# Fourth attention block: eight buffers for transposed P, and products by v ordered in front of MLP products

## The chip, the cores and the metric

The kernel runs on one core of one Trainium2 chip. The metric is the device time of the core in microseconds (us). TensorE does the matrix products, VectorE and ScalarE the elementwise work, GpSimd a few small operations and accumulating stores, and SyncE issues most of the loads and all the DMA transposes. Each engine works through its own queue in the order in which the program was scheduled.

## The reference

Inputs are q, k, v of shape (4, 8, 576, 64) and forget gates f of shape (4, 8, 576). Three layers follow each other:

```python
# 1: causal attention with a decay bias, per batch and head
scores = q @ k.T / 8 + (cum[:, None] - cum[None, :])      # cum = cumsum(log f)
attn = exp(masked scores - row max);  attn /= sum(attn) + 1e-9
x = concat_heads(attn @ v)                                 # (4, 576, 512)
# 2: MLP on the layer norm, with a residual
x = x + max(norm(x) * g @ w1, 0) @ w2                      # 512 -> 2048 -> 512
# 3: gated unit with mixing over positions
u, v = split(max(x @ w_in, 0));  out = (u * (w_spatial @ norm(v) + b)) @ w_out
```

## The kernel before

The 2304 tokens (4 batches of 576) are cut into nine blocks of 256 token columns. Blocks 1 and 2 hold the first 128 positions of two batches each, blocks 3 and 4 positions 128 to 255 of two batches each, blocks 5 to 8 the rest of one batch each, and the ninth column block gathers what is left over. For each block the attention runs, then its normalization, then the MLP. The MLP runs in eight groups of blocks: group 0 for block 1, group 1 for block 2, and so on. Each group has 16 steps, one for each tile of 128 hidden units: the first-layer product of step j into a bank `ph` (L864), a ReLU into `hh` (ScalarE, L875) and the low half `hl` (VectorE, L879), and then the second-layer product of the hidden tile two steps back into `acc` (function `second`, L849). From group 1 on, each product is taken as three fp16 products of high and low halves: 12 matmuls a step in each layer. There are two `ph` banks and three `hh`/`hl` buffers.

The attention of blocks 3 and 4 is `attention1`. Its unit is a head pair and a batch: eight units a block. A unit loads q/k, decay rows and v (L523 to L525), computes scores (L532), a row minimum with the mask (VectorE, L537), the exponential (ScalarE, L539), the reciprocal (L541), normalized P as high and low fp16 halves (L544 and L546), transposes P by one DMA on SyncE's queue (L547, the transposes kept in order among themselves), takes the product by v, 12 matmuls (L555), and writes the result into `xT` (ScalarE, L556). Buffers of each kind come from a dictionary: `BUFS1` for block 3, `BUFS1B` for block 4 (`self.deep` is set before block 4).

The order of the work is made in two stages. `run` gives each step of each block's attention and of each MLP group a time on a common axis and emits them in the order of these times; block 4 (the fourth entry of SPAN, 1.04 to 1.36) is emitted beside group 1 (1.0 to 1.5). Then the scheduler of the language takes the instructions with its own estimates of durations: on each engine, the earliest emitted one that it believes ready. That makes the fixed order of each engine's queue. `self.after(later, earlier)` adds an edge that only constrains this order.

Of the kernel before, what the change touches and what calls it, by code (L numbers as in the profile page):

```python
# [27 lines left out]
SC = 2.0 ** 14  # L28
BUFS = dict(vr=1, vp=2, qk=3, x1=3, x2=3, PT=4, sd=3, st=6, P16=5, xt=1)
BUFS0 = dict(vr=1, qk=1, e=4, diag=2, PT=2, st=4)  # L30
BUFS1B = dict(vr=4, vp=4, qk=4, sd=4, P16=4, PT=3, st=8)
BUFS1 = dict(vr=3, vp=3, qk=3, sd=2, P16=2, PT=2, st=6)
DHE = (0, 0, 0)
MB = dict(xT=4, xh=8, hh=3, y=2)
# [5 lines left out]
AHEAD = 2  # L40
# [39 lines left out]
def f32(ap):  # L80
    return ap.bitcast(F32)
# [7 lines left out]
class Kernel:  # L89
# [422 lines left out]
    def attention1(self, b, xT):  # L512
        nc, at, bufs = self.nc, self.at, BUFS1B if self.deep else BUFS1
        mm = nc.tensor.matmul
        for p in range(NP):
            for n in range(2):
                ph = at.tile([P, 2, 2, 2, P], F16, tag="P16", name="P16", bufs=bufs["P16"])
                PT = at.tile([P, 2, 2, 2, P], F16, tag="PT", name="PT", bufs=bufs["PT"])
                vr = at.tile([P, 2, P], F32, tag="vr", name="vr", bufs=bufs["vr"])
                vp = at.tile([P, 2, 2, P], F16, tag="vp", name="vp", bufs=bufs["vp"])  # L520
                qk = at.tile([66, 2, 3 * P], F32, tag="qk", name="qk", bufs=bufs["qk"])
                h = b * H + 4 * p + n
                nc.sync.dma_start(out=qk[:64], in_=self.qk1[b + n, p, :64])  # L523
                nc.sync.dma_start(out=qk[64:], in_=self.decay1_d[h : h + 3 : 2].rearrange("u r s -> r u s"))
                load = nc.sync.dma_start(out=vr, in_=self.v[b + n, : 2 * P, p * P : (p + 1) * P].rearrange("(t p) d -> p t d", p=P))  # L525
                if n:
                    self.marks.setdefault("second", load)
                vsc = self.parts16(vr, vp[:, 0], vp[:, 1], b + n if self.deep else None)
                yield
                ps = self.bank("s").rearrange("p (u k) -> p u k", u=2)  # L530
                for u in range(2):
                    mm(ps[:, u], lhsT=qk[:, u, :P], rhs=qk[:, u, P:], start=True, stop=True, skip_group_check=True)  # L532
                sd = at.tile([P, 2, 2 * P], F32, tag="sd", name="sd", bufs=bufs["sd"])
                st = at.tile([P, 4], F32, tag="st", name="st", bufs=bufs["st"])
                for u in range(2):
                    mn, sm = st[:, u : u + 1], st[:, 2 + u : 3 + u]
                    nc.vector.tensor_tensor_reduce(  # L537
                        out=sd[:, u], in0=ps[:, u], in1=self.mask[:, 3 * P :], scale=-0.125, scalar=3e38, op0=ALU.add, op1=ALU.min, accum_out=mn)
                    nc.scalar.activation(sd[:, u], sd[:, u], AF.Exp, bias=mn, scale=-1.0, accum_out=sm)  # L539
                nc.scalar.activation(st[:, 2:], st[:, 2:], AF.Copy, bias=1e-9 / SC, scale=1.0 / SC)  # L540
                nc.vector.reciprocal(st[:, 2:], st[:, 2:])  # L541
                for u in range(2):
                    rs, src = st[:, 2 + u : 3 + u], sd[:, u].rearrange("p (t w) -> p t w", w=P)
                    dh, dl = ph[:, u, :, 0], ph[:, u, :, 1]  # L544
                    self.copy(0, dh, src, rs)
                    nc.vector.scalar_tensor_tensor(out=dl, in0=src, scalar=rs, in1=dh, op0=ALU.mult, op1=ALU.subtract)  # L546
                tr = nc.sync.dma_start_transpose(out=PT.rearrange("p u t h w -> p (u t h) w"), in_=ph.rearrange("p u t h w -> p (u t h w)"))  # L547
                self.in_order("tr", tr)
                yield
                pav = self.bank("av")[:, :P]  # L550
                terms = [(kt, vi, pi) for kt in range(2) for vi, pi in ((0, 1), (1, 0), (0, 0))]
                for g, (kt, vi, pi) in enumerate(terms):
                    for u in range(2):
                        us = slice(64 * u, 64 * u + 64)
                        mm(pav[us], lhsT=vp[:, vi, kt, us], rhs=PT[:, u, kt, pi], start=g == 0, stop=g == len(terms) - 1, skip_group_check=True)  # L555
                nc.scalar.activation(xT[:, p, n * P : (n + 1) * P], pav, AF.Copy, scale=vsc)  # L556
                if n == 0:
                    yield
            if p == 1:
                xs = self.mo_sum(xT)  # L560
            elif p == 2:
                nc.vector.tensor_tensor(out=xs, in0=xs, in1=xT[:, 2, :], op=ALU.add)
            yield
        return xs
# [249 lines left out]
    def mlp(self, g, states, y):  # L814
# [19 lines left out]
        def weight(j, c0, right):  # L834

            cs = slice(c0, c0 + P)
            if not g:
                return [(self.wt[:, j + 2, cs], right)]
            h, l = self.pair(j)
            rh, rl = right  # L840
            return [(l[:, cs], rh), (h[:, cs], rl), (h[:, cs], rh)]

        def second(j, hidden, last):
            for m in range(NK):

                bank = m if n > 1 else m // 2
                terms = weight(j, DM + m * P, hidden)
                for e, (a, b) in enumerate(terms):
                    ins = nc.tensor.matmul(acc[m], lhsT=a, rhs=b, start=bank not in clear, stop=last and e == len(terms) - 1, skip_group_check=True)  # L849
                    if bank not in clear:  # L850
                        clear[bank] = ins
                    elif m not in seen and not e:
                        self.after(ins, clear[bank])
                    seen.add(m)

        pend = []
        for i in range(n):
            x = split(i)
        for j in range(NF):
            ph = self.bank("ph")[:, :W]  # L860
            for k in range(NK):
                terms = weight(j, k * P, (xn[k][0][:, :W], xn[k][1][:, :W]) if g else x[:, k, :])
                for e, (a, b) in enumerate(terms):
                    ins = nc.tensor.matmul(ph, lhsT=a, rhs=b, start=k == e == 0, stop=k == NK - 1 and e == len(terms) - 1)  # L864
                    if (g, j, k) == (0, SUMS, 0):
                        self.after(ins, self.marks["sums"])
            if g == 0:
                self.marks["hidden"] = ins
                for i in range(SQ[j - 1] if j else 0, SQ[j]) if j < len(SQ) else ():
                    self.squares(i)  # L870
            hh = mo.tile([P, 2 * TOK], F16, tag="hh", name="hh", bufs=MB["hh"])
            hl = mo.tile([P, 2 * TOK], F16, tag="hl", name="hl", bufs=MB["hh"])[:, :W] if g else None
            hh = hh[:, :W] if g else f32(hh)
            with self.tc.high_priority(1):
                relu = nc.scalar.activation(hh, ph, AF.Relu)  # L875
                if g < 2:
                    self.done.append(relu)
                if g:
                    nc.vector.scalar_tensor_tensor(out=hl, in0=ph, scalar=0.0, in1=hh, op0=ALU.max, op1=ALU.subtract)  # L879
            pend.append((j, (hh, hl) if g else hh, j == NF - 1))  # L880
            if j >= AHEAD:
                second(*pend[j - AHEAD])
            yield
        for args in pend[-AHEAD:]:
            second(*args)
# [400 lines left out]

    def run(self):
        self.setup()
        last = len(BLOCKS)
        ps_cm = self.banks("psum")  # L1290
        self.psum = ps_cm.__enter__()
# [170 lines left out]
        g, begun = self.mlp2(0), 0  # L1462
        for b in range(B):
# [12 lines left out]
            g = after  # L1476
# [57 lines left out]
```

## Time and profile before

| what | value |
|---|---|
| median of 3 runs (lowest, highest) | 764.69 us (762.89, 765.9) |
| profiled execution, its span | 763.16 us, 761.2 us |
| TensorE busy | 739.7 us (97%) |
| VectorE, ScalarE, GpSimd busy | 590.9, 528.8, 67.4 us |
| TensorE busy in 150 to 200 us | 49.64 of 50 us |
| TensorE busy in 250 to 300, in 300 to 350 us | 48.28, 46.36 of 50 us |
| DMA share in 150 to 200, in 300 to 350 us | 0.68, 0.96 |

An engine's busy time counts its instructions, not its waits. Matmuls are pipelined, so a row's busy time can reach into the next row's; the distance between two starts tells how long TensorE was taken. In a timeline row the bracket at the end holds the idle time before the row and what ended it. "x12" merges twelve neighbours of one kind.

### The profile page before, as it was taken

The page shows a single profiled execution, that of the slowest core. Times are in us where ns is not written, and L with a number is a line of the kernel's source. Part 1 is how long each engine was busy: PE and PEld are TensorE (multiplying, and loading weights), DVE is VectorE, ACT ScalarE, POOL GpSimd, SP SyncE. Part 2 cuts the span into 40 slices and gives each one's busy share as a digit, 9 for nine tenths or more (in the row PEclk, how much of TensorE's full clock was granted, in tenths as well). Part 3 has the DMA queues.
Part 4 walks back from the last instruction along what each step waited for, and adds up shares of the span by engine and source line. Part 5 has one row for each costly group of instructions (what it writes and reads, how often), then busy time and mean ns, then how long its engine had stood idle before and what let it go on. Part 6 is the DMA issues. An engine that isn't in the chain of part 4 may idle for free.

```text
span 761.2 us, 16265 instructions
## 1 busy us (share of the span) xinstructions
PE 739.7 (97%) x5912; PEld 567.9 (75%) x5912; DVE 590.9 (78%) x1569; ACT 528.8 (69%) x1320; POOL 67.4 (9%) x102
## 2 busy tenths in 40 slices
PE   8899998999999999999999999999999999999998
PEld 6788887888888877877888888644447678768686
DVE  7899799577599989989869845689456796785854
ACT  6898699576588989879857844587346764664633
POOL 6001100013102010110110100200012000000000
PEclk9999999999999999999999999999999999999999
DMA  8978694466589998988965944831025240100101
GB/s 263 295 269 274 206 266 84 89 171 105 176 167 206 198 220 183 195 189 177 201 144 116 148 84 149 213 132 56 1 22 111 70 125 1 44 21 7 57 2 62
DMA packets 164100, 104.68 MB, mean 138 GB/s; under 512 B 106147, under 2 KB 151299, under 8 KB 164021
## 3 DMA queue, kind: packets, MB, share of 16 engines
q1 hardware_dynamic: 153032, 93.06, 50.3%
q0 software_dynamic: 5376, 5.54, 5.2%
q10 hardware_dynamic: 5612, 5.06, 2.2%
q8 instruction: 46, 0.75, 0.4%
q14 instruction: 34, 0.27, 0.1%
HBM read 64.37 MB, written 15.11 MB: 104 GB/s over the span
## 4 chain that ended last, share of the span: by engine, by line
PE 63%; DVE 11%; ACT 10%; DMA 10%; issue 4%; SPq 2%; DVEq 0%; ACTq 0%
PE ph L864 16%; PE acc L849 12%; PE pb L808 8%; PE pb L809 8%; PE pb L810 8%; DMA raw<-in_moe_w_ch_dram 3%; PE s L359 3%; PE s L849 3%; DMA vr<-in_v_dram 2%; PE av L586 2%; ACT wt L744 2%; ACT P L319 2%; DMA x_d<-xT 2%; DVE P L380 1%; DMA qk<-decay 1%
## 5 line engine op out<-in xcount | busy, mean ns | idle before, releaser
L849 PE MATMUL acc<-hh,wt 128*128 128x256 f16 (+2 forms) x960 | 196.8, 295 | 3.2 <-ACT hh L875 3.2
L864 PE MATMUL ph<-xh,wt 128*128 128x256 f16 (+1 forms) x896 | 185.0, 288 | 2.0 <-DVE hl L879 2.0
L864 PEld LDWEIGHTS <-wt 128*128 128x128 f16 x1344 | 126.9, 98 | 47.4 <-issue 10.2
L849 PEld LDWEIGHTS <-wt 128*128 128x128 f16 x1344 | 128.7, 98 | 44.3 <-issue 5.3
L864 PE MATMUL ph<-xl,wt 128*128 128x256 f16 (+1 forms) x448 | 129.0, 288 | 0.0
L849 PE MATMUL acc<-hl,wt 128*128 128x256 f16 (+1 forms) x416 | 115.8, 281 | 1.1 <-DVE hl L879 1.1
L875 ACT ACTIVATE hh<-ph 128x256 f16<-128x256 f32 (+2 forms) x128 | 50.9, 397 | 45.8 <-PE ph L864 45.5
L879 DVE SCALAR_TENSOR_TENSOR hl<-ph,hh 128x256 f16<-128x256 f32 (+1 forms) x112 | 50.5, 453 | 35.9 <-ACT hh L875 35.7
L319 ACT ACTIVATE P<-sd,st 128x512 f16<-128x512 f32 (+2 forms) x128 | 70.6, 585 | 9.8 <-DVE st L370 6.9
L380 DVE SCALAR_TENSOR_TENSOR P<-sd,st,P 128x384 f16<-128x384 f32 (+2 forms) x96 | 59.2, 634 | 10.5 <-ACT P L319 10.3
L367 ACT ACTIVATE sd<-sd,st 128x384 f32<-128x384 f32 (+2 forms) x80 | 54.6, 682 | 14.4 <-DVE st L363 14.2
L359 PE MATMUL s<-x2z 128*128 128x384 f32 (+3 forms) x128 | 47.8, 382 | 1.9 <-DMA x2z<-decay_d 1.7
L363 DVE CUSTOM_DVE_ANT_0 sd<-s,mask 128x384 f32<-128x384 f32 (+2 forms) x80 | 46.0, 579 | 3.7 <-PE s L359 2.7
L900 POOL DMA_DIRECT2D x_d<-t x36 | 31.9, 1024 | 182.7 <-DVE t L896 153.1
L359 PE MATMUL s<-x 128*128 128x384 f32 (+3 forms) x128 | 41.4, 333 | 0.0
L809 PE MATMUL pb<-wsl,vh 128*128 128x288 f16 x128 | 36.6, 286 | 0.0
L808 PE MATMUL pb<-wsh,vl 128*128 128x288 f16 x128 | 36.6, 286 | 0.0
L810 PE MATMUL pb<-wsh,vh 128*128 128x288 f16 x128 | 36.4, 286 | 0.0
L810 PE MATMUL pb<-gh,woh 128*128 128x288 f16 x128 | 35.0, 286 | 0.0
L809 PE MATMUL pb<-gl,woh 128*128 128x288 f16 x128 | 35.0, 286 | 0.0
L808 PE MATMUL pb<-gh,wol 128*128 128x288 f16 x128 | 33.3, 286 | 0.0
L922 ACT ACTIVATE gh<-u 128x288 f16<-128x288 f32 x32 | 14.0, 437 | 26.5 <-DVE u L1261 26.5
(341 smaller groups left out, 1692.5 us busy)
## 6 DMA issues: line engine op xcount, KB each, us to landing
raw<-in_moe_w_ch_dram SPq DMA_DIRECT2D x32, 512.0 KB
qk<-in_qk_dram SPq DMA_DIRECT2D x32, 448.0 KB
vraw<-in_v_dram SPq DMA_DIRECT2D x5, 1024.0 KB
vr<-in_v_dram SPq DMA_DIRECT2D x16, 320.0 KB
x_d<-t POOLq DMA_DIRECT2D x36, 128.0 KB, 4.3
out_dram<-o SPq DMA_DIRECT2D x32, 144.0 KB
raw<-in_moe_w_in_dram SPq DMA_DIRECT2D x8, 512.0 KB
qk<-in_qk_dram SPq DMA_DIRECT2D x16, 192.0 KB
```

Of the source, the lines that this page charges most:

```text
L319: self.nc.scalar.activation(out, in_, AF.Copy, scale=scale)
L359: nc.tensor.matmul(ps[: R * u + R, : c1 - c0], lhsT=x[:, lo - q0 - R * u : hi - q0], rhs=y[:, c0:c1], start=g == 0, stop=g == len(heads[u] ...
L363: nc.vector.tensor_tensor_reduce(out=sd[:M, c0:c1], in0=ps[:M, : c1 - c0], in1=mask, scale=-0.125, scalar=3e38 if n == 0 else st[:M, n - 1 ...
L367: nc.scalar.activation(sd[:M, :N], sd[:M, :N], AF.Exp, bias=st[:M, n : n + 1], scale=-1.0, accum_out=st[:M, 2:3])
L380: low = nc.vector.scalar_tensor_tensor(out=dl, in0=src, scalar=rs, in1=dh, op0=ALU.mult, op1=ALU.subtract)
L808: first = mm(out, lhsT=al, rhs=bh, start=start, stop=False, **kw)
L809: mm(out, lhsT=ah, rhs=bl, start=False, stop=False, **kw)
L810: mm(out, lhsT=ah, rhs=bh, start=False, stop=stop, **kw)
L849: ins = nc.tensor.matmul(acc[m], lhsT=a, rhs=b, start=bank not in clear, stop=last and e == len(terms) - 1, skip_group_check=True)
L864: ins = nc.tensor.matmul(ph, lhsT=a, rhs=b, start=k == e == 0, stop=k == NK - 1 and e == len(terms) - 1)
L875: relu = nc.scalar.activation(hh, ph, AF.Relu)
L879: nc.vector.scalar_tensor_tensor(out=hl, in0=ph, scalar=0.0, in1=hh, op0=ALU.max, op1=ALU.subtract)
```

## The change

The fourth block gets eight buffers of transposed P in place of three. The last matmul of each of its products by v is remembered. At each MLP step the one remembered last is appended to a list of at most ten; in group 1 the first matmul of the second-layer products is placed behind the oldest entry of the list, that is, the product by v that had been emitted nine steps before. The full diff:

```diff
-BUFS1B = dict(vr=4, vp=4, qk=4, sd=4, P16=4, PT=3, st=8)
+BUFS1B = dict(vr=4, vp=4, qk=4, sd=4, P16=4, PT=8, st=8)
...
                     for u in range(2):
                         us = slice(64 * u, 64 * u + 64)
-                        mm(pav[us], lhsT=vp[:, vi, kt, us], rhs=PT[:, u, kt, pi], start=g == 0, stop=g == len(terms) - 1, skip_group_check=True)
+                        ins = mm(pav[us], lhsT=vp[:, vi, kt, us], rhs=PT[:, u, kt, pi], start=g == 0, stop=g == len(terms) - 1, skip_group_check=True)
+                if self.deep:
+                    self.summed1 = ins
...
-        def second(j, hidden, last):
+        def second(j, hidden, last, trail=()):
...
+                    if m == e == 0 and trail and trail[0] is not None:
+                        self.after(ins, trail[0])
...
             if j >= AHEAD:
-                second(*pend[j - AHEAD])
+                self.trail = [*self.trail, self.summed1][-10:]
+                second(*pend[j - AHEAD], self.trail if g == 1 else ())
...
         self.setup()
+        self.summed1, self.trail = None, []
```

## Rows read from the trace of the kernel before

**Rows 1.** Page, busy us, share of the span, instructions of TensorE
```profile
PE 739.7 (97%) x5912; PEld 567.9 (75%) x5912; DVE 590.9 (78%) x1569; ACT 528.8 (69%) x1320; POOL 67.4 (9%) x102
```
**Rows 2.** Busy time by stretch: stretch, length, each engine, granted clock, DMA share, GB/s
```profile
157.28:179.50 22.22, 21.86 (x181) 18.09 (x179) 21.20 (x76) 20.85 (x72) 2.05 (x2) 1.00 0.62 141
200.00:350.00 150.00, 143.93 (x1294) 117.80 (x1292) 135.98 (x371) 131.60 (x341) 15.43 (x24) 1.00 0.92 188
```
**Rows 3.** TensorE timeline, waits of 200 to 350 us: start, busy, instruction, [idle, releaser]
```profile
218.93 0.27 PE L864 MATMUL ph<-xh,wt 128*128 128x256 f16 x1 [0.71 <-DVE hl L879]
...
268.40 0.30 PE L586 MATMUL av<-PT,vp 128*64 128x320 f16 x1 [1.68 <-DMA PT<-P]
...
301.92 0.27 PE L849 MATMUL acc<-hl,wt 128*128 128x256 f16 x1 [1.11 <-DVE hl L879]
...
324.55 0.30 PE L586 MATMUL av<-PT,vp 128*64 128x320 f16 x1 [1.04 <-DMA PT<-P]
...
348.41 0.41 PE L359 MATMUL s<-x2z 128*128 128x384 f32 x1 [1.49 <-DMA x2z<-decay_d]
```
**Rows 4.** TensorE timeline of the fourth block beside group 1
```profile
157.28 0.27 PE L849 MATMUL acc<-hh,wt 128*128 128x256 f16 x1
...
157.61 1.03 PE L532 MATMUL s<-qk 66*128 66x256 f32 x4
...
172.45 0.53 PE L555 MATMUL av<-PT,vp 128*64 128x128 f16 x12
...
173.68 0.27 PE L849 MATMUL acc<-hh,wt 128*128 128x256 f16 x1
...
184.07 0.53 PE L555 MATMUL av<-PT,vp 128*64 128x128 f16 x12
...
196.80 0.53 PE L555 MATMUL av<-PT,vp 128*64 128x128 f16 x12
```
**Rows 5.** VectorE timeline, low half of P of units 1, 4 and 8
```profile
163.37 0.88 DVE L546 SCALAR_TENSOR_TENSOR P<-sd,st,P 128x256 f16<-128x256 f32 x2 [0.24 <-ACT P L319]
...
171.00 0.88 DVE L546 SCALAR_TENSOR_TENSOR P<-sd,st,P 128x256 f16<-128x256 f32 x2
...
181.48 0.87 DVE L546 SCALAR_TENSOR_TENSOR P<-sd,st,P 128x256 f16<-128x256 f32 x2
```
**Rows 6.** SyncE timeline: transposes of the fourth block, first loads of the fifth
```profile
164.28 1.24 SPq L547 DMA_TRANSPOSE PT<-P  x1
...
169.14 19.90 SPq L547 DMA_TRANSPOSE PT<-P  x6
189.14 1.01 SPq L330 DMA_DIRECT2D qk<-in_qk_dram  x2
```
**Rows 7.** SyncE and TensorE timelines, third block: a transpose and its product
```profile
126.52 1.89 SPq L547 DMA_TRANSPOSE PT<-P  x1
...
130.00 0.53 PE L555 MATMUL av<-PT,vp 128*64 128x128 f16 x12 [0.58 <-DMA PT<-P]
```
**Rows 8.** Waits of SyncE's queue, 150 to 260 us: total us, times, longest
```profile
SPq L547 <- PE av L555: 8.6, 4, 3.0
```
**Rows 9.** ScalarE timeline: a ReLU of group 1, first operands of the fifth block
```profile
165.51 0.36 ACT L875 ACTIVATE hh<-ph 128x256 f16<-128x256 f32 x1
...
199.06 0.94 ACT L319 ACTIVATE x<-qk 128x896 fp32r<-128x896 f32 x1
```
**Rows 10.** TensorE and VectorE timelines: third block's last product, a held subtraction
```profile
151.14 0.53 PE L555 MATMUL av<-PT,vp 128*64 128x128 f16 x12
...
156.97 1.41 DVE L782 TENSOR_TENSOR xT<-xT,av 128x256 f32<-128x256 f32 x4 [1.70 <-DMA x_d<-xT]
```
**Rows 11.** Chain that ended last, in order of time: start, us, work
```profile
135.56 0.97 PE s L532 x4
...
179.65 1.31 PE ph L864 x12
180.96 0.46 PE av L555 x12
```

## The prediction

> **What bounds the kernel now.** I read the page's busy times first. TensorE is busy 739.7 of 761.2 us [rows 1], so all its idle time together is 21.5 us, and no reordering can give back more. The profiled execution took 763.16 us, 1.96 us more than its span; the median of the runs shown is 764.69, so the profiled execution lies 1.5 us (0.2%) below it, near the fastest run.
>
> Then I looked for the part of the idle time that lies where the change can reach, in the busy times by stretch. From the point where the fourth block's scores begin to the end of the MLP group that runs beside it, TensorE is busy 21.86 of 22.22 us: 0.36 us idle. VectorE (21.20) and ScalarE (20.85) are almost as full, because there the fourth block's softmax runs at full speed. From 200 to 350 us, where the four wide attention blocks run, TensorE is busy 143.93 of 150 [rows 2]. TensorE's timeline names the five waits that make up nearly all of these 6.07 us: 0.71, 1.68, 1.11, 1.04 and 1.49, together 6.03, of which 4.21 are waits for DMAs (transposed P twice, rows of x2z once) [rows 3]. So the fourth block itself has nothing to give. A gain has to come from the blocks behind it.
>
> Third, the timeline of the fourth block. TensorE's queue holds its score matmuls from 157.61 on, but its eight products by v stand far behind: the first at 172.45, the fourth at 184.07, the eighth at 196.80, one per MLP step at the end [rows 4]. They wait for nothing there. P of the first unit is finished at 163.37 + 0.88 = 164.25, of the fourth at 171.88, of the eighth at 182.35 [rows 5], and SyncE starts the first transpose at 164.28 [rows 6]. How long a transpose takes until its product can run is seen in the third block, where the product did wait: issued at 126.52, product at 130.00, so 3.5 us [rows 7]. The first product could have run at 167.8 and the eighth near 185.9. The order of the queue, not the data, makes them late.
>
> What these late products hold back is SyncE. With three buffers of transposed P, the fourth transpose waits for the first product, and so on: four waits of 8.6 us in all [rows 8]. The last six transposes occupy SyncE's in-order queue from 169.14 to 189.04, and the first load of the fifth block (L330) stands behind them at 189.14 [rows 6]. ScalarE starts on the fifth block's operands at 199.06, just after the last product [rows 9].
>
> **The change part by part.** *Eight buffers.* There are eight units (four head pairs, two batch halves), so no transpose waits for a product any more. SyncE is through when P of the eighth unit is ready and its transpose issued: 182.35 + 1.3 = 183.7 in place of 189.0, so the loads of the fifth block can be issued 5.4 us earlier. One unit of transposed P is 2 KB per partition, so the pool grows by 10 KB, and by the order of allocation the fourth block's q/k tiles come to lie on tiles of the third block's pool. Their first load then waits for the third block's last product (151.14 + 0.53) rather than standing before it. I cost that at nothing: VectorE is held until 156.97 by the store of an earlier block's xT [rows 10], and the softmax stands behind that instruction. Without that cover the load would still land near 155.2 (151.7 + 3.5, taken like a transpose), before the first scores at 157.61.
>
> *The order edges.* They concern MLP group 1 alone, from the point where the list of ten holds a product. From the code: a product is emitted every third of the block's 27 events, MLP steps every 0.0294; so the list's oldest entry is product 1 at step 12 and products 2 to 4 at steps 13 to 15. Steps run two behind, so the first matmul of the second-layer products of hidden tiles 10 to 13 may not stand in front of products 1 to 4. Products 5 to 8 have no edge. Counting 12-matmul steps back from the end of the group, tile 10 began at 157.28 and tile 13 at 173.68 [rows 4]. Products 1 to 4 stood at 172.45 to 184.07: all four edges are broken in the order of before, so the order has to change by 10 to 15 us of TensorE's queue.
>
> The cost on the chip is what TensorE has to do between 157.28 and the moment when product 1 can run, 167.8: 10.5 us. An MLP step half (12 matmuls) is 1.31 us, a product by v 0.46, a unit's scores 0.97 [rows 11]. In front of product 1 can stand: seven units of scores (6.8), the first-layer tiles 13 and 14, which have two PSUM banks to fill (2.6), and the 9 matmuls of each of tiles 10 to 12 that no edge holds (only the first output quarter is tied; 3 x 0.98 = 2.9). That is 12.3, over 10.5, so I expect no wait at product 1. Behind it come the rest of tile 10 (0.33), product 2, the rest of 11, the eighth scores (0.97), product 3 (data at 169.14 + 3.5 = 172.6), the rest of 12: TensorE stands at about 173.4. Product 4's data come at 171.88 + 3.5 = 175.4. What fills the hole is late next: hidden tile 13 needs the buffer of tile 10 (three buffers), free only at about 171, and the ReLU that writes it, at 165.51 before [rows 9], now goes into ScalarE's queue among softmax work that keeps ScalarE over 90% busy. I place it near the fifth unit's P, about 174.5. So 1.1 us of idle there, and 0.2 more at tiles 14 and 15: **+1.3 us**. Nearest below: no wait at all and the 0.36 gone (-0.4). Nearest above: the three last ReLUs stand behind the whole softmax (182.35), and the group, which ended at about 179.5, ends one ReLU, one subtraction (0.7 for two instructions like that of [rows 9]) and a step half (1.31) after it, at 184.4: +5.0. I take 1.3 because the ReLUs have priority over the softmax once they are ready.
>
> *The blocks behind.* The fifth block's loads come 5.4 us earlier, its operands when the eighth product is done, perhaps 6 us earlier. TensorE's queue also asks for its scores earlier, by an amount no row shows (0 to the 10.4 us by which tile 13 preceded product 4). Of the 4.21 us of DMA waits I count a quarter as gone: **-1.0 us**. Bounds: -6.0 if all five waits of [rows 3] go, +3.4 if two more like the longest (1.68) appear, since the whole order behind is drawn anew.
>
> Sum: 763.16 + 1.3 - 1.0 = 763.5, on the median's footing 765.0; I give the middle, **764.2 us**.
>
> **Rivals.** (a) *TensorE stalls at the ordered products.* One mechanism: in-order TensorE stands before a second-layer step whose product, or whose hidden tile, is late, because ScalarE's queue has softmax of units five to eight in front of the ReLUs of tiles 13 to 15. For it: ScalarE and VectorE have only 1.4 and 1.0 us free in 22.2 [rows 2]. Against it: the ReLU has priority. It decides when the last ReLU comes after about 182; price 5.0 us, with nothing won behind: on the median's footing 769.7. A page of the Trainium skill speaks against the change here. "TensorE: Matmul & The Clock Gate", section "What's actually happening", says that the array's default state is half rate and that activity lifts it, so a long stall could bring the clock down. In this trace the granted clock is 1.00, the 2.4 GHz level, in both stretches of [rows 2], the one with the 1.68 us wait included, so the trace does not bear it out. By that rule a pair of step halves would cost 2.6 us more and this rival would reach some 772; I give it 2 chances in 100 of its own, inside this rival's chance.
>
> (b) *The early fifth block wins.* Its operands come about 6 us earlier, attention runs ahead of the MLP that fills TensorE, and four fifths of the 6.03 us go, with the stage at its lower end: -4.8 - 0.2, so 759.7 on the median's footing. For it: 4.21 of the 6.03 us are waits for attention's own DMAs [rows 3], which an earlier start would let land in time. Against it: VectorE is busy 136 of 150 us there [rows 2], so the attention is short of throughput, and a head start is worth only itself.
>
> (c) *The order hardly matters.* TensorE's work is unchanged and its queue refills itself; both terms are near zero: 763.2 to 764.7.
>
> **How the numbers follow.** My forecast and (c) hold 0.54 together, (a) 0.23, (b) 0.23. About 0.5% (3.8 us) is what a measurement of this kernel can tell from no change: 760.9 and 768.5. Nearly all of (b) with little more gives faster 0.23; (a) slower 0.23; the same 0.54. The likeliest case's own range is 761.5 to 768. Taking in most of both rivals the range is 758.5 to 770.5; its low end is -6.0 with the stage's -0.2 from the median, its high end +5.0 with a little of the redrawn order.
>
> **What would show it.** Right: the four tied products stand before 177 us in TensorE's queue, with one or two short waits for a ReLU's tile between 172 and 178; no SyncE wait of a transpose for a product; the fifth block's first load at about 184; the operand copies of the fifth block before 195. Wrong: TensorE idle over 4 us between 157 and 190; or the fifth block's loads still near 189; or the sum of waits from 200 to 350 below 2 or above 9 us.

## The result, and the profile after

The changed kernel takes 770.12 us (median of 5 runs, 769.53 to 771.67) against 764.69 us (5 runs, 761.21 to 765.9): 1.0084 times as long, 95% interval 1.0056 to 1.0112. It is slower by more than a measurement's noise. The profiled execution took 770.42 us with a span of 768.7.

The page after, first its busy times, then TensorE's granted clock in 40 slices (9 is full rate):

```profile
PE 747.4 (97%) x5912; PEld 573.9 (75%) x5912; DVE 593.6 (77%) x1569; ACT 529.5 (69%) x1320; POOL 67.2 (9%) x102
...
PEclk9999999998999999999999999999999999999999
```

TensorE has the same 5912 matmuls as in [rows 1] and is busy 7.7 us longer: that is not more work, it is (all but some 0.7 us) work at a lower clock. The busy times by stretch show where (columns as in [rows 2]):

```profile
157.35:184.30 26.95, 25.28 (x197) 19.50 (x196) 23.20 (x80) 23.50 (x78) 2.06 (x2) 0.87 0.69 145
...
200.00:350.00 150.00, 143.76 (x1292) 117.83 (x1291) 135.04 (x362) 128.11 (x329) 15.22 (x24) 0.99 0.89 185
169.00:178.00 9.00, 8.05 (x55) 5.48 (x56) 7.62 (x24) 7.93 (x28) 0.00 (x0) 0.62 0.68 105
```

The stretch from the first scores to the end of MLP group 1 was 22.22 us long and had 0.36 us idle [rows 2]; now it is 26.95 us up to the group's first output copy (its last matmul starts at 184.67), 1.67 of it idle, and the mean granted clock is 0.87. From 169 to 178 us it is 0.62, so most of that stretch ran at the lower level, 1.2 GHz. TensorE's timeline shows what came ahead of it:

```profile
166.59 1.03 PE L532 MATMUL s<-qk 66*128 66x256 f32 x4
...
168.00 0.27 PE L851 MATMUL acc<-hh,wt 128*128 128x256 f16 x1
169.95 1.73 PE L532 MATMUL s<-qk 66*128 66x256 f32 x4 [1.67 <-DVE st L541]
171.61 0.85 PE L555 MATMUL av<-PT,vp 128*64 128x128 f16 x12
...
173.78 0.85 PE L555 MATMUL av<-PT,vp 128*64 128x128 f16 x12
...
178.51 0.53 PE L555 MATMUL av<-PT,vp 128*64 128x128 f16 x12
...
181.69 0.53 PE L555 MATMUL av<-PT,vp 128*64 128x128 f16 x12
...
194.42 0.53 PE L555 MATMUL av<-PT,vp 128*64 128x128 f16 x12
```

TensorE waits 1.67 us at the eighth unit's scores, and what comes next takes longer: four score matmuls 1.73 us in place of 1.03, a product by v 0.85 in place of 0.53. Product 1, which the first edge was to bring forward, stands behind those scores: it ran at 171.61, against 172.45 in [rows 4]. Product 4 came forward from 184.07 to 181.69, the eighth from 196.80 to 194.42. The group's first output copy is at 184.33, against 179.20 before. Here is what the eighth scores wait for, in SyncE's queue:

```profile
163.42 1.24 SPq L547 DMA_TRANSPOSE PT<-P  x1
164.71 0.57 SPq L525 DMA_DIRECT2D vr<-in_v_dram  x1
165.38 1.24 SPq L547 DMA_TRANSPOSE PT<-P  x1
166.71 0.56 SPq L523 DMA_DIRECT2D qk<-in_qk_dram  x1
167.32 0.44 SPq L524 DMA_DIRECT2D qk<-decay_d  x1
167.81 0.38 SPq L525 DMA_DIRECT2D vr<-in_v_dram  x1
168.30 14.80 SPq L547 DMA_TRANSPOSE PT<-P  x6
183.19 1.02 SPq L330 DMA_DIRECT2D qk<-in_qk_dram  x2
```

The eighth unit's q/k load stands behind the second transpose and is issued at 166.71; 2.2 us after the last of its two parts the scores run. (The row above names VectorE's L541 as releaser; in the second profile of the same kernel, below, the same wait is put down to this load.) SyncE is through with the transposes at 183.1 in place of 189.0 and the fifth block's loads follow at 183.19, as forecast. But ScalarE's first operand copy for that block came only from 199.06 to 195.81, behind product 8.

### The profile page after: what moved, and what is told of

Same layout as the page of the kernel before. It is cut to its first block, busy times and chain, and to the rows that moved or that the text cites. A ratio compares the mean times of both kernels' runs of the same rounds, so it can differ in the third digit from the quotient of the medians.

```text
span 768.7 us, 16241 instructions
## 1 busy us (share of the span) xinstructions
PE 747.4 (97%) x5912; PEld 573.9 (75%) x5912; DVE 593.6 (77%) x1569; ACT 529.5 (69%) x1320; POOL 67.2 (9%) x102
## 4 chain that ended last, share of the span: by engine, by line
PE 65%; DVE 12%; ACT 12%; DMA 7%; issue 3%; SPq 1%; DVEq 0%; ACTq 0%
PE ph L868 15%; PE acc L851 13%; PE pb L810 8%; PE pb L811 8%; PE pb L812 8%; PE s L359 3%; PE av L588 2%; DMA x_d<-xT 2%; ACT wt L746 2%; DMA vr<-in_v_dram 2%; DVE P L380 2%; PE s L851 1%; ACT P L319 1%; DVE x2z L342 1%; DMA raw<-in_moe_w_in_dram 1%
## 5 line engine op out<-in xcount | busy, mean ns | idle before, releaser
L868 PEld LDWEIGHTS <-wt 128*128 128x128 f16 x1344 | 129.4, 99 | 48.8 <-issue 10.9
L851 PEld LDWEIGHTS <-wt 128*128 128x128 f16 x1344 | 129.3, 99 | 45.1 <-issue 5.7
L367 ACT ACTIVATE sd<-sd,st 128x512 f32<-128x512 f32 (+2 forms) x80 | 54.6, 682 | 17.0 <-DVE st L363 16.7
```

Of the source, the lines that this page charges most:

```text
L367: nc.scalar.activation(sd[:M, :N], sd[:M, :N], AF.Exp, bias=st[:M, n : n + 1], scale=-1.0, accum_out=st[:M, 2:3])
```

## The experiments

Three theories were set against each other. (A) The loss lies where the edges act, beside the fourth block. (B) It lies in the order of blocks 5 to 8, which the edges redraw. (C) It comes from the eight buffers.

For all profiles I count the same work: from the first scores of the fourth block to the first mean of the ninth block, behind which every kernel with the edges has, but for a few matmuls, the queue order of before. "Lost" is TensorE's idle time plus what half rate costs, (1 - granted clock) x length, summed over stretches of 5 us. The labels are those of the experiments below: e0_again is the changed kernel unaltered; e1_eight has the buffers alone, e2_edges the edges alone; e3_lag11 and e3_lag10 have a list two and one entries longer; e4_s15 has the fourth edge alone; f1_early5 issues loads earlier; f2_fill14 adds matmuls in front of the eighth scores; the runs m add matmuls to the kernel before and the runs am to the changed kernel, in MLP group 2.

| kernel | length | idle + half rate to 200 us | 200 to 350 | 350 to end |
|---|---|---|---|---|
| before | 304.1 | 0.4 + 0 | 6.1 + 0 | 0.4 |
| e1_eight | 305.1 | 0 + 0 | 6.1 + 1.8 | 0.7 |
| e3_lag11 | 305.9 | 0.2 + 0 | 5.8 + 0 | 2.8 |
| changed | 311.4 | 1.7 + 3.5 | 6.2 + 1.7 | 1.2 |
| e0_again | 311.9 | 2.8 + 1.7 | 8.5 + 0 | 1.0 |
| e2_edges | 312.6 | 3.4 + 1.7 | 5.6 + 1.7 | 2.1 |
| f1_early5 | 312.0 | 2.0 + 1.7 | 8.3 + 0 | 2.2 |
| f2_fill14 | 310.1 | 1.6 + 0 | 8.7 + 0 | 1.0 |
| e4_s15 | 310.2 | 0.9 + 0 | 8.3 + 1.7 | 0.9 |
| e3_lag10 | 313.6 | 2.7 + 1.7 | 8.7 + 1.7 | 1.1 |
| m0_4 | 309.5 | 1.1 + 0 | 4.5 + 1.7 | 5.0 |
| m0_8 | 304.4 | 0.2 + 0 | 6.0 + 0 | 0.2 |
| m2_4 | 306.0 | 1.5 + 0 | 4.2 + 1.7 | 1.8 |
| m4_8 | 304.3 | 0.5 + 0 | 4.6 + 0 | 1.4 |
| am2_8 | 317.3 | 3.0 + 1.7 | 11.2 + 1.7 | 1.0 |
| am4_16 | 311.5 | 2.2 + 1.7 | 5.8 + 1.7 | 1.0 |
| am10_8 | 320.3 | 1.7 + 1.7 | 14.2 + 5.1 | 0.6 |

Length less lost is 296.1 to 298.4 us in all seventeen (matmuls added by an experiment taken off at 0.109 us each). So nearly the whole difference, all but about 2 us of up to 16, is idle time and half rate on TensorE.

**Which part of the change: buffers, edges, and the kernel again.** The changed kernel unaltered:

> The changed kernel once more. Theories: (A) the loss lies where the edges act: a wait of some 1.7 us at the eighth unit's scores, half rate of TensorE behind it, MLP group 1 ending 5 us later. (B) the loss comes from the order of blocks 5 to 8, which the edges redraw as a whole. (C) it comes from the eight buffers: SyncE runs ahead and its loads collide. All expect 769.5 to 771.5 here. If the half-rate stretches of the first profile (14 us in three places, 7 us lost) are what costs, the profile shows them again at the same places; if the time stays and they do not come again, the clock is not what sets the time.

Eight buffers alone:

```diff
-BUFS1B = dict(vr=4, vp=4, qk=4, sd=4, P16=4, PT=3, st=8)
+BUFS1B = dict(vr=4, vp=4, qk=4, sd=4, P16=4, PT=8, st=8)
```

> Eight buffers without the edges; every engine's queue has the order of before, only the waits of SyncE differ. (A) and (B) expect no change, 763 to 766, with SyncE free 5 us earlier and no wait of a transpose for a product. (C) expects 767 or more.

The changed kernel with three buffers:

```diff
-BUFS1B = dict(vr=4, vp=4, qk=4, sd=4, P16=4, PT=8, st=8)
+BUFS1B = dict(vr=4, vp=4, qk=4, sd=4, P16=4, PT=3, st=8)
```

> The edges with three buffers; every queue has the order of the changed kernel. (A) and (B) expect 769 to 772, at most 1.5 us over the changed kernel, because products 4 to 8 can wait for transposes that wait for buffers. (C) expects 763 to 766.

Measured against the kernel before: the changed kernel again 1.0116 (1.0068 to 1.0164); buffers alone 1.0009 (0.9984 to 1.0033); edges alone 1.0098 (1.0070 to 1.0126). The loss comes with the edges, with three buffers as with eight, and (C) falls. In the profile of the buffers alone no transpose waits for a product and the fifth block's loads are issued at 182.18, 7 us earlier than in [rows 6], with no effect on the time that these runs can tell: in the order of before, SyncE's lateness was off the critical path. In the second profile of the changed kernel the wait names its load:

```profile
170.05 1.10 PE L532 MATMUL s<-qk 66*128 66x256 f32 x4 [2.82 <-DMA qk<-in_qk_dram]
```

Half rate came again behind it (3.4 us long, 1.7 lost), but not at 317 us, where the first profile had it too. It also shows near 120 us, ahead of the block, in nine of the seventeen profiles, with either order.

**A longer list.** Two entries more, and one entry more:

```diff
-                self.trail = [*self.trail, self.summed1][-10:]
+                self.trail = [*self.trail, self.summed1][-12:]
```

> Eight buffers, the list two entries longer: product 1 in front of hidden tile 12 and product 2 in front of tile 13, no other edge. The order behind, from about 225 us on, is that of before; in front of the eighth scores TensorE has more first-layer work. (A) expects a short wait or none at the eighth scores, no half rate, and 763 to 766.5. (B) expects 763 to 766, since blocks 5 to 8 run in the old order. Were any early product by v bad in itself, it would be above 767.

```diff
-                self.trail = [*self.trail, self.summed1][-10:]
+                self.trail = [*self.trail, self.summed1][-11:]
```

> The list one entry longer: products 1 to 3 in front of hidden tiles 11 to 13. More MLP work stands in front of the eighth scores, so little or no wait there; the order behind is redrawn, and not as in the changed kernel. (A) 763 to 766. (B) anything a redraw gives; 767 or more would say that a redrawn order is in general worse than the one of before.

With 12 entries: 1.0007 (0.9985 to 1.0029), no change, product 1 at 171.47 and product 2 at 174.42 without a wait at the eighth scores. An earlier product by v is not bad in itself, and brings nothing. With 11: 1.0129 (1.0105 to 1.0153), the worst so far, with only 0.39 us at the eighth scores: 0.95 and 1.16 us at product 2 and a hidden tile took its place. (A) as a matter of that one wait falls.

**One edge alone**, the fourth:

```diff
-                second(*pend[j - AHEAD], self.trail if g == 1 else ())
+                second(*pend[j - AHEAD], self.trail if g == 1 and j == 15 else ())
```

> Only the edge of product 4 in front of hidden tile 13. In front of 177 us the order is that of before (no long wait at the eighth scores); from about 285 us on it is that of the changed kernel in every queue. (A) 763 to 766. (B) 767 to 771. If both terms are real (4.6 of the 7.3 us local, 2.7 in the redrawn order), 766 to 767.

1.0066 (1.0049 to 1.0083). Beside the fourth block it loses 0.9 us only, yet the group's last output copies are at 181.85 (before: 180.70), and it loses 10.0 us from 200 to 350 us (before: 6.1), in an order that is the changed kernel's from about 285 us on; 5.4 of the 10.0 are lost ahead of that. So a redrawn order can cost by itself, as (B) has it; how much of this is in the changed kernel's own order, this run does not tell.

**The wait at the eighth scores.** First, its loads issued earlier (with eight q/k buffers):

```diff
-BUFS1B = dict(vr=4, vp=4, qk=4, sd=4, P16=4, PT=8, st=8)
+BUFS1B = dict(vr=4, vp=4, qk=8, sd=4, P16=4, PT=8, st=8)
...
+        def fetch(i):
+            q, m = i // 2, i % 2
+            fetched[i] = t = at.tile([66, 2, 3 * P], F32, tag="qk", name="qk", bufs=bufs["qk"])
+            h = b * H + 4 * q + m
+            nc.sync.dma_start(out=t[:64], in_=self.qk1[b + m, q, :64])
+            nc.sync.dma_start(out=t[64:], in_=self.decay1_d[h : h + 3 : 2].rearrange("u r s -> r u s"))
...
+                if self.deep and 2 * p + n == 5:
+                    for i in range(5 + 1, 8):
+                        fetch(i)
```

> The changed kernel with the q/k loads of the last two units issued with those of the sixth unit (eight q/k buffers), so that they stand in front of the first transposes in SyncE's queue; the other queues keep the changed kernel's order (TensorE's but for one matmul). (A) The wait at the eighth scores (1.67 to 2.86 us, for the q/k load) goes, the half rate behind it (1.7 to 3.4 us lost) too: 4 to 5 of the 7.3 us come back, 765 to 767. If the wait only moves to the product behind it, for its PSUM bank, still 1.3 us come back. (B) The order of blocks 5 to 8 is the same, so the loss stays: 769 to 772.

1.0078 (1.0054 to 1.0102): no gain that these intervals can tell from none. The wait is gone, and two others stand in its place:

```profile
167.89 1.03 PE L543 MATMUL s<-qk 66*128 66x256 f32 x4
169.31 0.53 PE L566 MATMUL av<-PT,vp 128*64 128x128 f16 x12 [0.40 <-DVE t L811]
...
172.24 0.85 PE L566 MATMUL av<-PT,vp 128*64 128x128 f16 x12 [1.64 <-ACT xT L569]
```

Products by v have one PSUM bank. Product 1 waits until a norm has read it, product 2 until ScalarE has copied product 1 out. ScalarE's queue (same kernel) has softmax in front of that copy:

```profile
170.95 0.19 ACT L551 ACTIVATE st<-st 128x2 f32<-128x2 f32 x1
171.04 0.89 ACT L319 ACTIVATE P<-sd,st 128x256 f16<-128x256 f32 x2
171.84 0.35 ACT L569 ACTIVATE xT<-av,vsc 128x128 f32<-128x128 f32 x1
```

Product 1 was finished near 169.8 and was copied at 171.84. Half rate follows this wait as it followed the other. Second, matmuls on ones to keep TensorE busy through the wait:

```diff
+                for _ in range(14 if self.deep and (p, n) == (3, 1) else 0):
+                    mm(ps[:, 0], lhsT=self.ones.bitcast(BF16)[:, :P], rhs=self.ones.bitcast(BF16), start=True, stop=True, skip_group_check=True)
```

> The changed kernel with 14 matmuls on ones (1.5 us at full rate, results overwritten) in front of the eighth scores; everything else in the same order. They run while TensorE would wait, so they add nothing if the wait is 1.5 us or more. If the half rate behind the wait costs time, it goes and 1.7 to 3.4 us come back: 767 to 769. If half rate is hidden by waits behind it, or does not go, 770 to 772.

The 14 matmuls run from 167.05, a wait of 0.53 us is left, and the clock stays up (0.62 in the changed kernel):

```profile
169.00:178.00 9.00, 7.63 (x84) 5.97 (x85) 8.76 (x26) 9.00 (x31) 0.00 (x0) 1.00 0.72 102
```

The time is 1.0100 (1.0080 to 1.0119), inside what the changed kernel had. At full rate TensorE meets the next late tile sooner: 1.10 us of waiting for a hidden tile at 174.06, with ScalarE busy all nine microseconds. In this profile a part of the gain does last. The queue order is the changed kernel's, so the same matmuls can be compared: the first scores come at 156.29 (157.35 in the changed kernel), the eighth product at 191.92 (194.42), the first mean of the ninth block at 466.35 (468.79), so 1.4 of the 3.5 us that half rate had taken beside the fourth block are won, and kept to the end. A gain of 1.4 us is 0.2%, and this profile is that of the fastest of the four runs: the times do not show it.

**Is any redrawn order worse?** The kernel before with a few matmuls on ones in MLP group 2, so that the order beside the fourth block stays and the scheduler draws the one behind anew:

```diff
             ph = self.bank("ph")[:, :W]
+            for _ in range(4 if (g, j) == (2, 0) else 0):
+                nc.tensor.matmul(ph, lhsT=self.ones.bitcast(BF16)[:, :P], rhs=self.ones.bitcast(BF16)[:, :W], start=True, stop=True, skip_group_check=True)
```

> The kernel before with four matmuls on ones (0.44 us, overwritten) in front of the first step of MLP group 2, which starts near 179 us. Block 4 keeps its order; the order of everything from there to about 460 us is redrawn (some 1200 lines of difference in TensorE's queue, as many as in the changed kernel). (A) Nothing is lost but the 0.44 us: 763.5 to 765. (B) A redrawn order is in general worse than the one that this kernel has been tuned on: 766 to 770.

> The same with eight matmuls (0.87 us): another redraw. (A) 764 to 765.5. (B) 766 to 770, and not the same as with four.

> Four matmuls in front of the third step of group 2: another redraw, from about 186 us on. (A) 763.5 to 765. (B) 766 to 770.

> Eight matmuls in front of the fifth step of group 2: another redraw, from about 193 us on. (A) 764 to 765.5. (B) 766 to 770.

In this order they measured 1.0079 (1.0050 to 1.0108), 1.0008 (0.9981 to 1.0035), 1.0013 (0.9991 to 1.0034), 0.9981 (0.9959 to 1.0004). One of four redraws costs as much as the change, three cost nothing. So a redraw is, by these four, a lottery of about 0 to 6 us, not a loss as such.

**The changed kernel's order beside the fourth block, with other orders behind:** the same lines put into the changed kernel, with 8 matmuls at step 2, 16 at step 4, 8 at step 10 of group 2.

> The changed kernel with eight matmuls on ones (0.87 us) in front of the third step of MLP group 2, near 190 us: the order beside the fourth block stays that of the changed kernel, the order behind is redrawn (some 900 lines). If the loss beside the fourth block (A, 4.5 us by the profiles) is a loss for the whole kernel, no redraw behind brings it back: 768 to 773. If the redrawn order behind is what costs (B), redraws behind scatter from 764 to 771 as they did behind the kernel before.

> The same with 16 matmuls (1.75 us) in front of the fifth step of group 2: another redraw (some 950 lines). (A) 769 to 774. (B) 765 to 772.

> The same with 8 matmuls in front of the eleventh step of group 2: another redraw (some 770 lines). (A) 768 to 773. (B) 764 to 771.

1.0137 (1.0094 to 1.0180), 1.0079 (1.0045 to 1.0114), 1.0182 (1.0153 to 1.0211); the added matmuls are 0.1 to 0.2% of that. None comes back to the kernel before. The fastest of them lost 3.9 us beside the fourth block and 8.5 us behind it, where the kernel before loses 6.5. So nothing behind made the loss beside the fourth block good again, as (A) has it, and a redraw comes on top. Three draws support this; they do not prove it for every order.

## Why the prediction was wrong

It forecast no change, +0.3 us, and the span grew by 7.5. Both terms of its sum failed. The time, 770.12 us, lies just inside the range that went up to 770.5, but by luck: that end was drawn for rival (a), whose late ReLUs are not what happened.

*The stage beside the fourth block: +1.3 forecast, +4.1 to +4.8 measured* (idle and half rate up to 200 us: 1.7 + 3.5, 2.8 + 1.7 and 3.4 + 1.7 in changed, e0_again and e2_edges, against 0.4 in the kernel before). The step that failed is the one that filled TensorE from 157.28 to product 1 and found 12.3 us of work for 10.5, hence no wait. It priced product 1 by when its own data arrive, 167.8, and placed the eighth scores behind product 2, with no wait of their own. The queue has the eighth scores in front of product 1 (whose data, by the same 3.5 us, were there at 166.9), and they wait for a load that SyncE issues at 166.71 behind the second transpose. Load and scores were no earlier in the kernel before:

```profile
167.57 0.55 SPq L523 DMA_DIRECT2D qk<-in_qk_dram  x1
...
170.76 1.10 PE L532 MATMUL s<-qk 66*128 66x256 f32 x4 [0.36 <-DVE st L541]
```

What changed is the work that covers the load. Between the start of hidden tile 10 and the wait TensorE had 13.12 us of work before (157.28 to 170.40) and has 11.26 us now (157.02 to 168.28). In front of the eighth scores stood 35 second-layer matmuls of tiles 10 to 12, and 18 stand there now: 17 x 0.109 = 1.85 us, which is the whole difference. The scores waited there before too, 0.36 us; that wait was counted and its cause not followed. Its length varies in the order of before as well, from 0 to 1.5 us (1.06 in m0_4, 1.48 in m2_4); in the six profiles with the edges of the change and no help for these scores it is 1.7 to 2.9 us. The count of 9 free matmuls a tile was wrong: 6 ran ahead, and the quarter that shares a PSUM bank with the tied one stayed behind with it. The step's own times also hold a wait of 0.5 us for product 3 (reached at 172.1, data at 172.6) that the +1.3 leaves out. Nor did it see that products brought together share one PSUM bank, and that ScalarE frees it behind softmax: that is the 1.64 us of f1_early5, once the load is out of the way.

*The clock* was given 2 chances in 100 inside rival (a). It fell in every profile with this order but that of f2_fill14, behind a wait of 1.6 to 2.9 us. The rule of the Trainium skill ("TensorE: Matmul & The Clock Gate", "What's actually happening"), that the array's default is half rate and activity lifts it, agrees with these falls, such as the 0.62 granted from 169 to 178 us; "not borne out" was concluded from one 1.68 us wait at full rate in [rows 3]. With the same order and eight buffers that product waited a little longer, and the clock fell behind it:

```profile
267.51 0.30 PE L586 MATMUL av<-PT,vp 128*64 128x320 f16 x1 [1.97 <-DMA PT<-P]
```

```profile
268.00:272.00 4.00, 4.00 (x33) 2.55 (x33) 2.82 (x8) 1.83 (x6) 0.20 (x1) 0.57 0.80 165
```

The time of that kernel did not change by more than its interval, which 1.7 us (0.2%) would fit into. Against the same matmuls of [rows 3], e1_eight is 0.89 us ahead at this product, 0.28 behind at the one of 301.92 and 0.18 ahead at the one of 348.41: 0.7 us were left there of the 1.7 that half rate took, the rest had come back in shorter waits. So the clock did fall, and in this profile its price is smaller than the time it lost; on the time of the whole kernel no run here resolves it.

*The blocks behind: -1.0 forecast, +0.7 to +2.8 measured* (from 200 us on 9.1 to 9.5 us lost in changed, e0_again and e2_edges, against 6.5, 8.6 and 8.6 in before, e1_eight and e3_lag11, which keep the order of before). The head start was 5.9 us on SyncE, as forecast, but 3.2 and not 6 us on ScalarE, which started behind product 8, and TensorE's queue did not profit: the waits of [rows 3] are gone or shorter and others stand in their place, such as

```profile
280.07 0.27 PE L868 MATMUL ph<-xh,wt 128*128 128x256 f16 x1 [0.39 <-DVE hl L883]
...
287.43 0.41 PE L359 MATMUL s<-x2z 128*128 128x384 f32 x1 [0.47 <-DMA x2z<-decay_d]
...
317.59 0.37 PE L868 MATMUL ph<-xh,wt 128*128 128x256 f16 x1 [1.58 <-DVE hl L883]
```

Counting a quarter of the DMA waits as gone had no ground in a row. What the redraws show is a spread, 6.0 to 11.2 us lost from 200 us on behind the order of before, 8.5 to 19.9 us behind the orders with edges that cost something. Why the second spread lies higher is open. In those runs, but for e4_s15, the first output copy of group 1 comes 25.4 to 27.5 us after the first scores, against 21.0 to 22.9 in the others, so the MLP work that fills TensorE lags behind the attention; that this is the cause was only argued.

*What held.* All four edges were broken in the order of before. The buffers take all waits of transposes for products away, free SyncE 6 to 7 us earlier, and cost nothing that shows by their place in memory. Rival (a) named the right place and nearly the right size, 5.0 us, but by another cause: it has late products or ReLUs behind softmax, with the last ReLU after 182, and the changed kernel waits for a q/k load. Softmax in ScalarE's queue, in front of the copy of a product, is the cause only in f1_early5. Rival (b), with as large a chance, did not come about: the loads were 7 us earlier in e1_eight and the operands 3.2 us earlier in the changed kernel, and neither won anything; operands 6 us earlier, as it supposed, no run gave. Of the signs, products 3 and 4 did not stand before 177 (178.51 and 181.69), yet none of those for "wrong" came: TensorE idled 1.7 to 3.4 us up to 200 and waited 5.6 to 8.5 us from 200 to 350, because matmuls at half rate do not count as idle.

## What to carry to other kernels

When an edge moves an instruction in an in-order queue, price the whole queue in front of it: each instruction that now stands ahead has its own loads and banks, and the latest of them sets the time, not the moved instruction's own data. In a kernel at 97% of its bounding engine, an edit that makes the scheduler draw 300 us anew has a spread of its own (here -0.2 to +0.8%), which belongs into the range; small neutral edits measure it. A resource freed earlier (SyncE by 6 to 7 us) is a gain only if something on the critical path waited for it.

## What the runs showed of the hardware that was not expected

TensorE's granted clock falls to half behind single waits of 1.35 us (e4_s15, at 241.41) to 4.16 us (am10_8, at 332.6), in kernels that keep it 96 or 97% busy, and not every time: 1.93 us (f2_fill14, at 335.10) and even 3.35 us (am10_8, at 282.03) left it at 1.00, and at one and the same product a wait of 1.68 us (kernel before) left it there and one of 1.97 us (e1_eight) did not. Half rate lasted 3.4 us in most places (1.7 us lost), and 6.8 us at 170 us in one profile of the changed kernel. Profiles of that kernel whose lost clock time was 7.0 and 3.4 us had spans of 768.7 and 768.3 us: the second one idled more.
